# Block 2's inverse: norms earlier on VectorE, column steps on GpSimd

## The chip, the cores and the metric

The kernel runs on one core of a Trainium2 chip. The metric is device microseconds of one launch. TensorE (PE in the profile, PEld for its weight loads), VectorE (DVE), ScalarE (ACT), GpSimd (POOL) and SyncE (SP) each work through a queue of their own in order, and wait for each other by semaphores.

## The reference

Two stages follow each other: a delta-rule attention over 768 time steps for 32 (batch, head) pairs, and a mixture of experts that sends each token to one of 8 experts.

```python
k_n = k / (np.linalg.norm(k, axis=-1, keepdims=True) + 1e-06)
for t in range(S):                                   # S = 768, state is [4, 8, 48, 48]
    y[:, :, t] = np.einsum('bhd,bhde->bhe', q[:, :, t], state)
    v_old = np.einsum('bhde,bhd->bhe', state, kt)
    state = state + bt[:, :, :, None] * np.einsum('bhd,bhe->bhde', kt, vt - v_old)
# x = y as 3072 rows of 384
expert_idx = np.argmax(x @ w_gate, axis=1)
h = np.maximum(xe @ w1[e], 0.0)                      # for the rows xe of expert e
out[mask] = gate_w[mask, None] * (h @ w2[e])
```

## The kernel before

**Blocks and ticks.** The 768 steps are cut into 6 blocks of 128 (`NT`), tb = 0 to 5, and each block into four sub-blocks of 32. Inside a sub-block the recurrence becomes a triangular system, whose 32 x 32 inverse is needed for every pair and sub-block: 4 x 32 = 128 inverses in a block, one in each partition. The main loop runs over 27 ticks t (24 units of one batch of one block, and three to drain). In a tick four units are in flight, each at another of its four sub-blocks. A block's inverse must stand in the tile `wt` when its first unit enters, at tick 4 tb.

**A tick.** `residual(t)` multiplies keys with the state and with the rows just made (TensorE, L434 and L446, into `ks`); VectorE subtracts the result from `v_all` (L453); `apply(t)` multiplies by the inverses `wt` (TensorE, L461); ScalarE copies the result to `u` (L465); the next residual reads `u`. Around this chain stand the Gram matrices of later units (`kpart`, L271, `gg`), the queries' products (`qpart`: L281 on ScalarE, a mask L282 on GpSimd), outputs and states (`finish`), the gate's logits (`emit_x`, L528 to L530), the rows' scaling `scale_v` (L417 on VectorE) and the tokens' places (`pool_slots`, small GpSimd instructions, from the fifth tick on).

**The inverse of a block.** The diagonal 32 x 32 pieces of the Gram matrices go through DRAM (`gd`, L259, L263) into the tile `lg`. Then, on VectorE but for the square root:
- `squares` (L295) and `root` (L299, ScalarE): the keys' squared norms and their square roots;
- `prepare` (L317 to L341): nine short instructions, one on another, that make the norms and scale `lg`, with a copy of the norms by GpSimd (L346);
- 15 column steps (L369 for the first, then 14 pairs of L374, a product into `tmp`, and L377, its addition to `lw`) for the two 16 x 16 triangles on the diagonal;
- the corner: a copy (L382), six large products (L393, 784 to 1024 elements in each partition) and six sums (L399), which join the triangles, and the transpose into `wt` (L404).

**What sets the order.** All instructions are recorded by one Python program, and every engine runs its share in that order. A tick has seven places, and `beside(t, i)` runs at each (place number 7t + i). It records `squares` and `root` at the places that the first two numbers of `ROOT[tb]` name, and then inverse steps worth `SPEND` (0.86 to 0.92 us a place, by the program's own weights). Block tb's `prepare` may begin at the third number of `ROOT[tb]`. Where two blocks are under way the steps alternate between them, until the older one has its corner. What a block still lacks at tick 4 tb is recorded there, ahead of `residual`.

Of the kernel before, what the change touches and what calls it, by code (L numbers as in the profile page):

```python
# [13 lines left out]
ALU = mybir.AluOpType  # L14
# [27 lines left out]
def deltanet_moe(ctx, tc, kt_d, qt_d, kn_d, v_d, beta_d, w_gate, w1, w2, out):  # L42
    nc = tc.nc
# [76 lines left out]

    ROOT = {1: (-1, -1, -1), 2: (17, 20, 22), 3: (38, 41, 43), 4: (66, 69, 71), 5: (94, 97, 99)}
    INIT = (0, 1, 2, 3, 'l', 0)
# [233 lines left out]

    def lanes(tb):

# [3 lines left out]
        G, W = both_halves(lg), both_halves(lw)  # L362
        V = nc.vector
        tmp = fp.tile([128, 128], F32, name=f"tmp{tb}", tag=f"tmp{tb % 2}")
        for c in range(15):
            m, w = 15 - c, c + 1
            if c == 0:
                for g in (0, 16):
# [4 lines left out]
            x = tmp[:, 0:2 * m * w].rearrange("p (g a b) -> p g a b", g=2, a=m)  # L373
            V.tensor_tensor(out=x, in0=G(w, c, m, 1).broadcast_to([128, 2, m, w]),  # L374
                            in1=W(c, 0, 1, w).broadcast_to([128, 2, m, w]), op=ALU.mult)
            yield 0.2 + m * w / 480
            V.tensor_tensor(out=W(w, 0, m, w), in0=W(w, 0, m, w), in1=x, op=ALU.add)  # L377
            yield 0.2 + m * w / 480
        big = [fp.tile([128, 1024], F32, name=f"big{i}_{tb}", tag=f"big{i}") for i in range(2)]

# [24 lines left out]
        if tb + 2 < NT:  # L405
            clear_w(tb + 2)
        yield 2.0

    def scale_v(t, act=False):
# [524 lines left out]
    class Inverse:  # L934
# [6 lines left out]
        def steps(self):  # L941
            for _ in prepare(self.tb):
                yield 0.2
            yield 1.2
            self.at = 0
            yield from lanes(self.tb)

        def ready(self, t):
            if self.at == -12:
                return place[0] >= ROOT[self.tb][2]  # L950
            return not ("cols" in tiles[self.tb] and t < B * self.tb - 1)

        def step(self):
# [5 lines left out]
            return us  # L959

    line = [Inverse(tb) for tb in range(1, NT)]
    turn, owed, place = [None], [0.0], [-1]
# [6 lines left out]
    W = None  # L969

    def inverse_step(t):
# [7 lines left out]
        pair = ready and b is not None and "cols" not in tiles[a.tb]  # L979
        x = (b if turn[0] is a else a) if pair else a if ready else b  # L980
        turn[0] = x
# [18 lines left out]
    def beside(t, i):  # L1000

        place[0] = 7 * t + i
        for tb in ROOT:
            if place[0] == ROOT[tb][0]:
                squares(tb)
            if place[0] == ROOT[tb][1]:
                root(tb)
        inverses((SPEND0 if t < B else SPEND if t < 3 * B else SPEND2)[i], t)
        for _ in range(STEPS[i] if t < NN - B else 4):
            if fine and not run(fine[0]):  # L1010
                fine.pop(0)
# [343 lines left out]
```

## Time and profile before

| | us |
|---|---|
| median of 3 runs (lowest, highest) | 497.71 (496.09, 498.83) |
| profiled execution | 496.72 |
| its span in the trace | 495.0 |
| ticks 0 to 3 (40.59 to 70.12) | 29.53 |
| ticks 4 to 7 (70.12 to 105.64) | 35.52 |
| all ticks until the last subtraction (40.59 to 257.70) | 217.11 |
| the experts behind them (257.70 to 495.00) | 237.30 |
| busy over the span: PE, DVE, ACT, POOL | 453.5, 323.8, 262.1, 166.1 |

A tick is counted here from one L453 to the next, since each tick has one such instruction (some of the first and last have a narrower form). Busy PE time is modelled from pipelined matmuls; its idle time, with the engine that ended it in square brackets behind a row, is the surer number. An instruction that is held up by another engine's use of the memory shows as a longer instruction, not as idle time.

### The profile page before, as it was taken

The page shows a single profiled execution, that of the slowest core. Times are in us where ns is not written, and L with a number is a line of the kernel's source. Part 1 is how long each engine was busy: PE and PEld are TensorE (multiplying, and loading weights), DVE is VectorE, ACT ScalarE, POOL GpSimd, SP SyncE. Part 2 cuts the span into 40 slices and gives each one's busy share as a digit, 9 for nine tenths or more (in the row PEclk, how much of TensorE's full clock was granted, in tenths as well). Part 3 has the DMA queues.
Part 4 walks back from the last instruction along what each step waited for, and adds up shares of the span by engine and source line. Part 5 has one row for each costly group of instructions (what it writes and reads, how often), then busy time and mean ns, then how long its engine had stood idle before and what let it go on. Part 6 is the DMA issues. An engine that isn't in the chain of part 4 may idle for free. (4 is left out here: it accounts for less than half of the span.)

```text
span 495.0 us, 17216 instructions
## 1 busy us (share of the span) xinstructions
PE 453.5 (92%) x7212; PEld 417.3 (84%) x7212; DVE 323.8 (65%) x726; ACT 262.1 (53%) x566; POOL 166.1 (34%) x338
## 2 busy tenths in 40 slices
PE   6866799999999899978899999999999999999995
PEld 4755678887888687866798999999999999999995
DVE  3899998899889989446544767373463647255330
ACT  3464767675756466766433455463553545364230
POOL 7013123768888878730311210201102020201111
PEclk9998889999999999999999899999999999999999
DMA  5999478575384243734302548474545547353101
GB/s 164 246 291 252 126 156 254 169 162 168 88 206 106 86 131 89 234 121 128 101 35 66 168 139 248 140 223 132 177 124 171 175 150 199 138 170 106 36 3 46
DMA packets 57147, 73.33 MB, mean 148 GB/s; under 512 B 25929, under 2 KB 44831, under 8 KB 57056
## 3 DMA queue, kind: packets, MB, share of 16 engines
q1 hardware_dynamic: 53600, 62.44, 44.4%
q0 software_dynamic: 3456, 9.57, 5.3%
q8 instruction: 71, 1.16, 1.0%
q14 instruction: 20, 0.16, 0.1%
HBM read 54.15 MB, written 18.62 MB: 147 GB/s over the span
## 5 line engine op out<-in xcount | busy, mean ns | idle before, releaser
L801 POOL DMA_INDIRECT out_dram<-yo,idx x32 | 30.7, 959 | 198.7 <-ACT yo L1134 100.8
L798 PE MATMUL y<-w2h,hx 128*128 128x384 f32 x352 | 93.5, 340 | 0.1
L721 DVE TENSOR_TENSOR w2l<-w2r,w2h 128x768 fp32r<-128x768 f32 x32 | 31.2, 979 | 73.3 <-ACT w2h L720 73.2
L798 PEld LDWEIGHTS y<-w2h,hx 128*128 128x128 f32 x352 | 64.1, 188 | 0.4 <-issue 0.4
L798 PE MATMUL y<-w2l,hx 128*128 128x384 f32 x176 | 59.3, 337 | 0.0
L787 PE MATMUL h<-xl,w1h 128*128 128x416 f32 (+2 forms) x168 | 57.2, 341 | 0.2 <-DVE xl L721 0.2
L787 PE MATMUL h<-xh,w1h 128*128 128x416 f32 (+2 forms) x168 | 57.3, 341 | 0.0
L787 PE MATMUL h<-xh,w1l 128*128 128x416 f32 (+2 forms) x168 | 57.2, 340 | 0.0
L465 ACT COPY u<-ks 32x384 f32<-32x384 f32 x96 | 45.1, 469 | 21.0 <-PE ks L461 18.4
L282 POOL TENSOR_SCALAR_AFFINE_SELECT pm<-pm 128x1024 f32<-128x1024 f32 x24 | 27.1, 1130 | 75.9 <-ACT pm L281 75.5
L790 ACT ACTIVATE hx<-h 128x448 fp32r<-128x448 f32 (+1 forms) x64 | 32.9, 517 | 32.8 <-PE h L787 32.0
L1134 ACT ACTIVATE yo<-y,gt 128x384 f32<-128x384 f32 x22 | 12.8, 581 | 69.1 <-PE y L798 57.9
L434 PE MATMUL ks<-st,kt 128*32 128x96 f32 x768 | 45.1, 253 | 2.5 <-ACT u L465 2.1
L791 DVE SCALAR_TENSOR_TENSOR hx<-h,hx 128x448 fp32r<-128x448 f32 (+1 forms) x64 | 36.8, 587 | 14.5 <-ACT hx L790 14.4
L271 PE MATMUL pg<-kt 64*128 64x128 f32 x384 | 34.0, 319 | 8.0 <-DMA kt<-in_kt_dram 4.3
L271 PEld LDWEIGHTS pg<-kt 64*128 64x128 f32 x384 | 28.8, 219 | 12.4 <-ACT gg L253 6.4
L434 PEld LDWEIGHTS ks<-st,kt 128*32 128x32 f32 x768 | 33.2, 111 | 6.1 <-ACT u L465 2.6
L253 ACT COPY gg<-pg 128x512 f32<-128x512 f32 x48 | 25.8, 589 | 23.8 <-PE pg L271 23.8
L536 POOL DMA_INDIRECT xg<-row,sli x24 | 29.2, 1216 | 25.7 <-ACT yt L508 8.0
L461 PE MATMUL ks<-v_all,wt 32*32 32x48 f32 x1536 | 25.9, 203 | 12.9 <-DVE v_all L453 10.7
L461 PEld LDWEIGHTS ks<-v_all,wt 32*32 32x32 f32 x1536 | 21.3, 105 | 17.8 <-DVE v_all L453 12.6
L721 DVE TENSOR_TENSOR w1l<-w1r,w1h 128x1024 fp32r<-128x1024 f32 x24 | 29.4, 1224 | 9.8 <-ACT w1h L720 6.6
(197 smaller groups left out, 1040.5 us busy)
## 6 DMA issues: line engine op xcount, KB each, us to landing
w1r<-in_w_dram SPq DMA_DIRECT2D x24, 512.0 KB
w2r<-in_w_dram SPq DMA_DIRECT2D x32, 384.0 KB
xg<-zrow SPq DMA_DIRECT2D x7, 788.0 KB
kt<-in_kt_dram SPq DMA_DIRECT2D x17, 256.0 KB
xr<-xg SPq DMA_DIRECT2D x7, 591.0 KB
ku<-in_kn_dram SPq DMA_DIRECT2D x20, 192.0 KB
qt<-in_qt_dram SPq DMA_DIRECT2D x36, 96.0 KB
v_all<-in_v_dram SPq DMA_DIRECT2D x15, 192.0 KB
```

Source lines behind the costliest of these rows:

```text
L271: nc.tensor.matmul(pg[a][:, p], lhsT=kt[r, p], rhs=xt[r, p], start=True, stop=True, tile_position=(64 * a, 0), skip_group_check=True)
L282: nc.gpsimd.affine_select(out=pm, in_=pm, compare_op=ALU.is_gt, fill=0.0, base=0, pattern=[[0, H], [1, C]], channel_multiplier=-1)
L434: nc.tensor.matmul(ks[32 * q:32 * q + 32, 2 * p:2 * p + 2, :], lhsT=kt_t[n % KTL][:, p, 32 * q:32 * q + 32], rhs=st_view(n % B, p), start= ...
L461: nc.tensor.matmul(ks[r, h, :], lhsT=tiles[n // B]["wt"][r, n % B * H + h, :], rhs=vn[r, h, :], start=True, stop=True, tile_position=(32 * ...
L465: nc.scalar.copy(out=uview(n)[r], in_=ks[r])
L536: put = nc.gpsimd.indirect_dma_start(out=xg, out_offset=bass.IndirectOffsetOnAxis(ap=at, axis=0), in_=x, in_offset=None, bounds_check=OFF ...
L721: nc.vector.tensor_tensor(out=lo, in0=src, in1=hi.bitcast(F32), op=ALU.subtract)
L787: nc.tensor.matmul(ps, lhsT=w[:, d, fs], rhs=x_[:, d], start=(n == 0), stop=(n == len(terms) - 1))
L790: nc.scalar.activation(out=hh, in_=ps, func=AF.Relu)
L791: nc.vector.scalar_tensor_tensor(out=hl, in0=ps, scalar=0.0, in1=hh.bitcast(F32), op0=ALU.max, op1=ALU.subtract)
L798: nc.tensor.matmul(ps, lhsT=h(f)[h_], rhs=w2[w][:, f, :], start=(n == 0), stop=(n == len(terms) - 1))
L801: nc.gpsimd.indirect_dma_start(out=out, out_offset=bass.IndirectOffsetOnAxis(ap=idx, axis=0), in_=yo, in_offset=None, bounds_check=N - 1, ...
```

## The change

Block 2's `squares`, `root` and `prepare` come in tick 1, some ten places earlier than before, and while they last they are always taken ahead of the older block's steps. Its column steps 1 to 14 are recorded for GpSimd, two instructions at each place from place 13 (tick 1's last) on; its corner stays on VectorE and isn't recorded before place 29, tick 4's second. Blocks 3, 4 and 5 get their squares at places 30, 58 and 88 (38, 66 and 94 before). Nothing else is touched: TensorE, ScalarE and the DMA queues have the same instructions, ScalarE's root (L299) of blocks 2 to 5 stands earlier.

```diff
--- before.py
+++ after.py
@@ -118,7 +118,8 @@
     LAG = NB - 1
     FILL = 'k4 k5 k6 k7', 'k1 q0 k2 k3', 'k8 k9', 'k10 k11 q1'
 
-    ROOT = {1: (-1, -1, -1), 2: (17, 20, 22), 3: (38, 41, 43), 4: (66, 69, 71), 5: (94, 97, 99)}
+    ROOT = {1: (-1, -1, -1), 2: (7, 9, 11), 3: (30, 32, 34), 4: (58, 61, 63), 5: (88, 91, 93)}
+    COLS = {2: (13, 2, 1, 29)}
     INIT = (0, 1, 2, 3, 'l', 0)
 
     STEPS = (3, 3, 3, 2, 2, 2, 2)
@@ -354,13 +355,13 @@
             return bass.AP(tensor=t.tensor, offset=t.offset + 32 * r + c, ap=[list(t.ap[0]), [16 * 33, 2], [32, m], [1, w]])
         return view
 
-    def lanes(tb):
+    def columns(tb):
 
 
         T = tiles[tb]
         lg, lw = T["lg"], T["lw"]
         G, W = both_halves(lg), both_halves(lw)
-        V = nc.vector
+        V, P = nc.vector, nc.gpsimd if tb in COLS else nc.vector
         tmp = fp.tile([128, 128], F32, name=f"tmp{tb}", tag=f"tmp{tb % 2}")
         for c in range(15):
             m, w = 15 - c, c + 1
@@ -371,11 +372,17 @@
                 yield 0.4
                 continue
             x = tmp[:, 0:2 * m * w].rearrange("p (g a b) -> p g a b", g=2, a=m)
-            V.tensor_tensor(out=x, in0=G(w, c, m, 1).broadcast_to([128, 2, m, w]),
+            P.tensor_tensor(out=x, in0=G(w, c, m, 1).broadcast_to([128, 2, m, w]),
                             in1=W(c, 0, 1, w).broadcast_to([128, 2, m, w]), op=ALU.mult)
             yield 0.2 + m * w / 480
-            V.tensor_tensor(out=W(w, 0, m, w), in0=W(w, 0, m, w), in1=x, op=ALU.add)
+            P.tensor_tensor(out=W(w, 0, m, w), in0=W(w, 0, m, w), in1=x, op=ALU.add)
             yield 0.2 + m * w / 480
+
+    def corner(tb):
+
+        T = tiles[tb]
+        lg, lw = T["lg"], T["lw"]
+        V = nc.vector
         big = [fp.tile([128, 1024], F32, name=f"big{i}_{tb}", tag=f"big{i}") for i in range(2)]
 
         first_, prod = lg[:, 0:16, 0:16], lg[:, 0:16, 16:32]
@@ -405,6 +412,10 @@
         if tb + 2 < NT:
             clear_w(tb + 2)
         yield 2.0
+
+    def lanes(tb):
+        yield from columns(tb)
+        yield from corner(tb)
 
     def scale_v(t, act=False):
 
@@ -943,11 +954,18 @@
                 yield 0.2
             yield 1.2
             self.at = 0
-            yield from lanes(self.tb)
+            if self.tb in COLS:
+                held[self.tb] = columns(self.tb)
+                yield next(held[self.tb])
+                yield from corner(self.tb)
+            else:
+                yield from lanes(self.tb)
 
         def ready(self, t):
             if self.at == -12:
                 return place[0] >= ROOT[self.tb][2]
+            if self.tb in COLS and (self.tb in held or place[0] < COLS[self.tb][3]) and self.at == 1:
+                return False
             return not ("cols" in tiles[self.tb] and t < B * self.tb - 1)
 
         def step(self):
@@ -958,6 +976,15 @@
             self.at += 1
             return us
 
+    def columns_beside():
+
+        for tb in list(held):
+            n = ((place[0] - COLS[tb][0] + 1) * COLS[tb][1]) // COLS[tb][2] - ((place[0] - COLS[tb][0]) * COLS[tb][1]) // COLS[tb][2]
+            for _ in range(n if place[0] >= COLS[tb][0] else 0):
+                if tb in held and next(held[tb], None) is None:
+                    del held[tb]
+
+    held = {}
     line = [Inverse(tb) for tb in range(1, NT)]
     turn, owed, place = [None], [0.0], [-1]
 
@@ -977,7 +1004,7 @@
         if not ready and b is None:
             return None
         pair = ready and b is not None and "cols" not in tiles[a.tb]
-        x = (b if turn[0] is a else a) if pair else a if ready else b
+        x = (b if turn[0] is a or (b.tb in COLS and b.at < 0) else a) if pair else a if ready else b
         turn[0] = x
         return x.step()
 
@@ -1006,6 +1033,7 @@
             if place[0] == ROOT[tb][1]:
                 root(tb)
         inverses((SPEND0 if t < B else SPEND if t < 3 * B else SPEND2)[i], t)
+        columns_beside()
         for _ in range(STEPS[i] if t < NN - B else 4):
             if fine and not run(fine[0]):
                 fine.pop(0)
```

The line numbers of the changed kernel are 1 higher than before up to the column steps, 7 higher in the corner and 11 higher from `scale_v` on. In the rows below lg_443, lw_161 and big_1 are block 1's tiles, lg_604 and lw_633 block 2's; `x2` marks two instructions of one form.

VectorE from tick 1 (its subtraction reads ks_702) to tick 2 (ks_783 before, ks_793 after), before:

```order
L374 TENSOR_TENSOR tmp_678<-lg_443,lw_161 128x78
L377 TENSOR_TENSOR lw_161<-lw_161,tmp_678 128x2x3x13
L374 TENSOR_TENSOR tmp_678<-lg_443,lw_161 128x56
L377 TENSOR_TENSOR lw_161<-lw_161,tmp_678 128x2x2x14
L374 TENSOR_TENSOR tmp_678<-lg_443,lw_161 128x30
L377 TENSOR_TENSOR lw_161<-lw_161,tmp_678 128x2x15
L382 COPY lg_443<-lw_161 128x16x16
L393 TENSOR_TENSOR big_1_778<-lg_443 128x1024
L453 TENSOR_TENSOR v_all<-v_all,ks_783 96x384
```

After:

```order
L375 TENSOR_TENSOR tmp_678<-lg_443,lw_161 128x78
L378 TENSOR_TENSOR lw_161<-lw_161,tmp_678 128x2x3x13
L318 RECIPROCAL r_722<-s_721 128x32
L320 SCALAR_TENSOR_TENSOR r_722<-ss_720,r_722 128x32
L322 SCALAR_TENSOR_TENSOR s_721<-r_722,s_721 128x32
L324 RECIPROCAL r_722<-s_721 128x32
L326 TENSOR_TENSOR ss_720<-bl,r_722 128x32
L329 TENSOR_TENSOR lw_633<-ss_720,r_722 128x32
L333 SCALAR_TENSOR_TENSOR lg_604<-lg_604,lw_633 128x16x16 x2
L342 STREAM_TRANSPOSE r_722<-s_721 128x32
L464 TENSOR_TENSOR v_all<-v_all,ks_793 96x384
L370 TENSOR_SCALAR lw_633<-lg_604,lw_633 128x15 x2
```

The nine instructions of block 2's norms stand inside block 1's column steps and ahead of tick 2's subtraction, and the first column step of block 2 right behind it. Block 1's last two column steps, its copy and its first product come behind that subtraction. Block 2's squares (L296, not in the piece) stand right behind tick 1's subtraction.

VectorE from tick 3's subtraction to tick 4's, before:

```order
L393 TENSOR_TENSOR big_1_778<-lw_161,lg_443 128x960
L317 RECIPROCAL r_869<-s_868 128x32
L399 TENSOR_REDUCE lw_161<-big_1_779 128x4x16
L319 SCALAR_TENSOR_TENSOR r_869<-ss_867,r_869 128x32
L393 TENSOR_TENSOR big_1_779<-lw_161,lg_443 128x784
L321 SCALAR_TENSOR_TENSOR s_868<-r_869,s_868 128x32
L399 TENSOR_REDUCE lw_161<-big_1_778 128x5x16
L323 RECIPROCAL r_869<-s_868 128x32
L399 TENSOR_REDUCE lw_161<-big_1_779 128x7x16
L325 TENSOR_TENSOR ss_867<-bl,r_869 128x32
L404 STREAM_TRANSPOSE wt_1060<-lw_161 128x32x32
L453 TENSOR_TENSOR v_all<-v_all,ks_1064 128x384
```

After:

```order
L464 TENSOR_TENSOR v_all<-v_all,ks_917 128x384
L406 TENSOR_REDUCE lg_443<-big_1_847 128x5x16
L406 TENSOR_REDUCE lg_443<-big_1_846 128x7x16
L400 TENSOR_TENSOR big_1_847<-lw_161,lg_443 128x1024
L400 TENSOR_TENSOR big_1_846<-lw_161,lg_443 128x960
L406 TENSOR_REDUCE lw_161<-big_1_847 128x4x16
L400 TENSOR_TENSOR big_1_847<-lw_161,lg_443 128x784
L406 TENSOR_REDUCE lw_161<-big_1_846 128x5x16
L406 TENSOR_REDUCE lw_161<-big_1_847 128x7x16
L411 STREAM_TRANSPOSE wt_1099<-lw_161 128x32x32
L464 TENSOR_TENSOR v_all<-v_all,ks_1103 128x384
```

Between the two subtractions stand one product and two sums of block 1 more than before, and none of block 2's norms. The transpose into block 1's `wt` stays the last instruction ahead of tick 4's subtraction.

GpSimd from tick 1 on, before:

```order
L346 COPY nt_all<-r_628 32x32 x4
L423 MEMSET u_735 128x384
L423 MEMSET u_826 128x384
L282 AFFINE_SELECT pm_118<-pm_118 128x1024
L423 MEMSET u_951 128x384
L282 AFFINE_SELECT pm_119<-pm_119 128x1024
L288 MEMSET lw_1062 128x1024
L346 COPY nt_all<-r_869 32x32 x4
```

After:

```order
L434 MEMSET u_739 128x384
L347 COPY nt_all<-r_722 32x32 x4
L375 TENSOR_TENSOR tmp_823<-lg_604,lw_633 128x56
L378 TENSOR_TENSOR lw_633<-lw_633,tmp_823 128x2x14x2
L434 MEMSET u_842 128x384
L375 TENSOR_TENSOR tmp_823<-lg_604,lw_633 128x78
L378 TENSOR_TENSOR lw_633<-lw_633,tmp_823 128x2x13x3
L375 TENSOR_TENSOR tmp_823<-lg_604,lw_633 128x96
L378 TENSOR_TENSOR lw_633<-lw_633,tmp_823 128x2x12x4
L375 TENSOR_TENSOR tmp_823<-lg_604,lw_633 128x110
L378 TENSOR_TENSOR lw_633<-lw_633,tmp_823 128x2x11x5
L375 TENSOR_TENSOR tmp_823<-lg_604,lw_633 128x120
```

Block 2's 28 column instructions (L375 and L378) stand in this queue with two of the masks (L283) and two of the `u` memsets (L434) among them; before, only masks and memsets stood there until tick 4.

## Rows read from the trace of the kernel before

**Rows 1.** Busy time by stretch (start:end, length, then each engine's busy time, PEclk, DMA).
```profile
40.59:70.12 29.53, 23.25 (x539) 20.28 (x540) 28.19 (x64) 19.07 (x59) 4.79 (x11) 0.83 0.67 158
70.12:105.64 35.52, 33.89 (x960) 29.41 (x958) 30.49 (x76) 24.22 (x59) 20.57 (x49) 1.00 0.70 195
78.08:94.80 16.72, 16.20 (x469) 13.98 (x470) 14.21 (x34) 11.75 (x29) 10.06 (x26) 1.00 0.70 210
94.80:113.24 18.44, 16.61 (x472) 14.31 (x472) 17.09 (x40) 11.62 (x28) 13.06 (x32) 1.00 0.68 158
146.14:160.91 14.77, 13.91 (x438) 12.22 (x439) 14.33 (x31) 9.60 (x25) 11.89 (x24) 1.00 0.50 139
160.91:177.47 16.56, 14.21 (x437) 12.14 (x437) 14.83 (x38) 9.58 (x24) 13.29 (x33) 1.00 0.33 101
64.00:66.00 2.00, 2.00 (x31) 1.90 (x29) 2.00 (x5) 1.93 (x6) 0.00 (x0) 0.50 1.01 155
```

**Rows 2.** Timeline of PE: start, busy us, instruction [idle before it <- who ended that].
```profile
62.61 0.88 PE L461 MATMUL ks<-v_all,wt 32*32 32x48 f32 x64 [2.03 <-DVE v_all L453]
...
71.93 0.88 PE L461 MATMUL ks<-v_all,wt 32*32 32x48 f32 x64
...
106.23 0.88 PE L461 MATMUL ks<-v_all,wt 32*32 32x48 f32 x64 [1.00 <-DVE v_all L453]
...
171.61 0.88 PE L461 MATMUL ks<-v_all,wt 32*32 32x48 f32 x64 [1.45 <-DVE v_all L453]
```

**Rows 3.** Timeline of DVE, ticks 0 to 4.
```profile
41.04 0.32 DVE L317 RECIPROCAL r<-s 128x32 f32<-128x32 f32 x1
...
42.53 0.22 DVE L328 TENSOR_TENSOR lw<-ss,r 128x32 f32<-128x32 f32 x1
...
44.01 0.24 DVE L374 TENSOR_TENSOR tmp<-lg,lw 128x56 f32<-128x56 f32 x1
...
47.93 0.28 DVE L374 TENSOR_TENSOR tmp<-lg,lw 128x128 f32<-128x128 f32 x1
...
62.01 0.54 DVE L453 TENSOR_TENSOR v_all<-v_all,ks 128x384 f32<-128x384 f32 x1
...
68.26 2.04 DVE L404 STREAM_TRANSPOSE wt<-lw 128x1024 f32<-128x1024 f32 x1
70.12 0.56 DVE L453 TENSOR_TENSOR v_all<-v_all,ks 128x384 f32<-128x384 f32 x1
```

**Rows 4.** Timeline of SP's DMA issues, tick 1.
```profile
48.72 0.35 SPq L191 DMA_DIRECT2D kt<-in_kt_dram  x1
```

**Rows 5.** SP's waits from 36 to 52 us: in total, times, longest.
```profile
SPq L191 <- DMA lg<-gd: 1.2, 1, 1.2
```

**Rows 6.** Timeline of POOL and DVE where both read the memory.
```profile
59.92 1.09 POOL L282 TENSOR_SCALAR_AFFINE_SELECT pm<-pm 128x1024 f32<-128x1024 f32 x1 [14.41 <-ACT pm L281]
59.94 2.15 DVE L393 TENSOR_TENSOR big<-lw,lg 128x1024 f32<-128x1024 f32 x1
...
150.16 2.29 DVE L393 TENSOR_TENSOR big<-lg 128x1024 f32<-128x1024 f32 x2
150.28 1.16 POOL L640 TENSOR_TENSOR s<-oh 128x8 f32<-128x8 f32 x1
```

**Rows 7.** Timeline of POOL: small two-input instructions, and a memset.
```profile
108.07 0.22 POOL L679 TENSOR_TENSOR oh<-oh,beyond 128x16 f32<-128x16 f32 x1
108.38 0.22 POOL L681 TENSOR_TENSOR pos<-oh,pos 128x16 f32<-128x16 f32 x1
...
108.83 0.42 POOL L423 MEMSET u<- 128x384 f32 x1
```

**Rows 8.** Groups of instructions by line: busy us, mean ns of one | idle before.
```profile
L282 POOL TENSOR_SCALAR_AFFINE_SELECT pm<-pm 128x1024 f32<-128x1024 f32 x24 | 27.1, 1130 | 75.9 <-ACT pm L281 75.5
...
L374 DVE TENSOR_TENSOR tmp<-lg,lw 128x56 f32<-128x56 f32 (+3 forms) x84 | 24.6, 293 | 2.5
...
L377 DVE TENSOR_TENSOR lw<-lw,tmp 128x56 f32<-128x56 f32 (+3 forms) x84 | 21.7, 258 | 2.5
...
L85 POOL CAST ltri<-cmask 128x128 bf16<-128x128 f32 x1 | 0.3, 289 | 0.1
```

## The prediction, made before the changed kernel ran

> **What bounds the kernel now.** I read the busy time by stretch first, then the idle gaps of TensorE in the timeline, then VectorE's timeline ahead of each gap, and last the places where VectorE and GpSimd work at once.
>
> The stretches [rows 1] show two regimes. In ticks 0 to 3 VectorE is busy 28.19 of 29.53 us and TensorE only 23.25; GpSimd does 4.79. VectorE is still finishing block 1's inverse, which tick 4 needs. From tick 4 on TensorE is busy 33.89 of 35.52 us, so that only its idle time can be won. The idle that VectorE causes is in front of `apply` [rows 2]: 2.03 us at tick 3, none at tick 4, 1.00 at tick 8 and 1.45 at tick 16. Ticks 8 and 16 are where blocks 2 and 4 enter, and their transposes come late. At tick 4 there is a hidden margin: VectorE's subtraction starts at 70.12 and takes 0.56 [rows 3], but `apply` starts only at 71.93 [rows 2], since other matmuls stand ahead of it. So VectorE may be 71.93 - 70.68 = 1.25 us later at tick 4 at no cost, and after that TensorE pays in full.
>
> **The change part by part.**
>
> *Removed from VectorE.* 28 column instructions of block 2, 14 x (0.293 + 0.258) = 7.7 us [rows 8]. All of them stood in ticks 4 to 7, where VectorE is the engine that is waited for only at the end. With 7.7 us less there, and the norms of blocks 3 to 5 eight, eight and six places earlier, the transposes of blocks 2 and 4 are ready in time. What this gives back is TensorE's idle time at ticks 8 and 16, 1.00 + 1.45 = 2.45 us, by the gaps. By lengths it is more: ticks 7 and 8 together take 18.44 us against 16.72 for ticks 5 and 6 (1.72), and ticks 15 and 16 take 16.56 against 14.77 for 13 and 14 (1.79) [rows 1], 3.5 in all. I take the middle, -3.0.
>
> *Added ahead of block 1's transpose.* That chain on VectorE is nearly gapless until 70.12, so what is put into it moves tick 4.
> - (a) The end of block 2's norms and its first column step now come before it: in block 1 the same instructions took from 42.53 to 44.01 [rows 3], +1.5.
> - (b) The first five instructions of the norms were there already, but between large instructions; now they stand behind each other, each on the one before, as in block 1, where they took 42.53 - 41.04 = 1.49. If they were free before this adds 1.5, if equally dear 0. I take +0.5.
> - (c) The squares now stand right behind tick 1's subtraction, at 47.93 [rows 3]. They read `lg`, which comes by a DMA that SP waits for until 48.72 [rows 4, 5]. That is up to 0.8 of stall on VectorE. With the squares' own time I take +0.9.
> - (d) GpSimd's 28 instructions run while VectorE does block 1's last two column steps and six products, ten instructions with two inputs. The trace shows what happens when both read [rows 6]: the mask on GpSimd runs from 59.92 to 61.01, and the product that VectorE starts at 59.94 takes 2.15 instead of about 1.15 (two products back to back took 2.29). The other way round, a small GpSimd instruction that takes about 0.22 [rows 7] takes 1.16 beside a product. So they exclude each other. A GpSimd instruction of the new kind isn't in the trace. Below it stands the 16-element one at 0.22, above it memsets of 384 elements at 0.42 [rows 7]; a one-input instruction of 128 elements takes 0.289 and of 1024 1.13 [rows 8], which is 0.94 ns an element. The new ones have 30 to 128 elements, 95 in the mean, so I estimate 0.26 to 0.35, of which 0.1 to 0.3 keep VectorE out. Ten meetings at 0.25 are +2.5 (0 to 3.5).
> - (e) The 1.0 us that the mask cost the product at 59.94 may recur or not, since the mask now comes at another moment: -0.5 (0 to -1.0).
>
> The Trainium skill (SBUF — State Buffer, section Who interferes with whom) says that a VectorE instruction with two SBUF inputs contends with a GpSimd instruction that reads SBUF, that the loser waits for the whole instruction, and that a tensor_reduce never contends. The trace agrees [rows 6]; by the rule the six sums are free for GpSimd and (d) holds at its estimate, without it (d) would be 0.
>
> Sum: 1.5 + 0.5 + 0.9 + 2.5 - 0.5 = +4.9 us on VectorE at tick 4. The subtraction starts near 75.0 instead of 70.12, and less the margin of 1.25 `apply` comes 3.7 us later. Tick 3 itself changes little: there VectorE is later by (a) to (c) and part of (d), and earlier by the two sums and the product that have moved behind it.
>
> *What TensorE's longer waits cost besides.* After the 2.03 us gap at tick 3 the granted clock is 0.50 from 64 to 66 us [rows 1], that is 1.2 GHz. A gap of 2 to 3 us before tick 4 can bring the same a tick later, where TensorE is the bound. Such a stretch costs 0 (hidden) to 1.6 us; I take +0.6.
>
> *GpSimd's own queue.* Its steps start once VectorE has done the first column step, near 56. 28 instructions at 0.26 to 0.35, and 0.08 between two (108.07 to 108.38 for 0.22 [rows 7]), are 9.5 to 12 us; two masks and two memsets among them 2 x 1.13 + 2 x 0.42 = 3.1; six products hold one step each by up to 1.0, 6 at most. They end between 69 and 77. Block 2's corner starts with a copy that waits for the last of them, about 1.1 us after tick 4's subtraction, at 76.1. So I cost this wait at nothing, and it is the thinnest cover in the sum. Queued behind that copy are five products and sums, and tick 5's subtraction. The `u` memsets have a tick in hand, the masks three.
>
> Added up: +3.7 + 0.6 - 3.0 = +1.3 us. The profiled execution of 496.72 (span 495.0) becomes 498.0. The runs' median lies 1.0 above it at 497.71, so I predict 499.0.
>
> **The rivals.**
> - *GpSimd slips in for nothing.* For it: the small instructions ran at 0.22 with VectorE's column steps beside them [rows 7]. Against it: they have 16 elements, and the mask of 1024 did block. Then (d) is 0, `apply` is late by 4.9 - 2.5 - 1.25 = 1.2, no new gap lowers the clock, and the sum is 1.2 - 3.0 = -1.8: 495.9. With a stall in (c) of nothing as well it reaches 495.
> - *GpSimd is the bound of tick 5.* If a two-input step with short rows takes 0.5 us, 28 x 0.58 + 3.1 + 6 = 25.3 us, the steps end at 81.3 and the copy waits 5.2 us; 1.2 of it is hidden as at tick 4. The sum is 1.3 + 4.0 = +5.3: 503.0. It decides from about 0.36 a step on. For it: the masks in the same queue and the products that hold it; against it: the 0.94 ns an element [rows 8].
>
> The Trainium skill (GPSIMD Engine Reference, section 3.1) gives 4497 ns for a two-input instruction of 2048 elements. Worked out from that page my estimate is 0.2 us for 95 elements beside the fixed part, some 0.4 in all, which would put the end of the steps at 78.5 and the sum at +2.5. No run here shows such an instruction.
> - *The gains are hidden anyway.* If what waits at ticks 8 and 16 is taken over by another wait (the masks that block VectorE, or GpSimd's small instructions for the tokens), the -3.0 shrinks to -0.5 and the sum is +3.8: 501.5. For it: ticks 15 and 16 also contain a mask's collision; against it: VectorE has 7.7 us less to do in ticks 4 to 7.
>
> **How the numbers follow.** Half a per cent, 2.5 us, is what a measurement of this kernel can tell from no change; so faster means under 495.2 and slower over 500.2. The forecast has 0.45, with a range of its own from 497 to 501; GpSimd for nothing 0.25, GpSimd as the bound 0.15, hidden gains 0.15. Faster: half of the second case and, by the spread of the runs, a little of the first, 0.16. Slower: most of the last two and a quarter of the first, 0.36. The same: 0.48. The range from 495 to 503.5 takes in the ends of (d), the second case and most of the others.
>
> **What would show it.** In the profile after: VectorE's products and column steps of block 1 in ticks 2 and 3 longer than 1.15 and 0.29 us where a GpSimd column step overlaps them; tick 4's subtraction near 75 instead of 70.1; a TensorE gap of 2 us or more before `apply` at tick 4, and none at ticks 8 and 16; the copy L389 of block 2 with little idle time before it. I am wrong if the subtraction of tick 4 starts before 73, if the copy waits more than 1.5 us for GpSimd, or if gaps at ticks 8 or 16 stay.

## The result, and the profile after

The changed kernel took 505.76 us (median of 6 runs, 502.54 to 509.72) beside 498.27 for the kernel before: ratio 1.0141, 95% interval 1.0099 to 1.0184. Timed again on another occasion (12 runs) it was 1.0072 (1.0031 to 1.0113). So it is slower, by about 1% or 5 us; predicted were 499.0 us, +0.3%, and 505.76 lies outside the range of 495 to 503.5. The profiled execution after took 502.54 (span 500.8) against 496.72 (495.0); it is the fastest of the six runs, so the trace shows less than the median's loss.

The stretches that answer to [rows 1], in the same columns (length, then PE, PEld, DVE, ACT, POOL busy, PEclk), the last one for TensorE's clock behind tick 4:

```profile
40.74:75.17 34.43, 25.76 (x576) 22.68 (x576) 30.40 (x71) 21.12 (x62) 19.21 (x37) 0.83 0.60 148
75.17:110.66 35.49, 31.44 (x913) 27.32 (x913) 28.66 (x60) 21.75 (x53) 22.56 (x51) 0.95 0.67 181
85.94:102.47 16.53, 14.20 (x445) 12.26 (x446) 13.16 (x30) 10.36 (x26) 11.83 (x28) 1.00 0.48 150
102.47:120.32 17.85, 17.27 (x486) 15.21 (x488) 13.92 (x36) 12.12 (x30) 11.86 (x28) 1.00 0.69 167
153.17:167.41 14.24, 13.15 (x429) 11.21 (x430) 12.32 (x26) 8.90 (x22) 10.86 (x26) 1.00 0.44 130
167.41:183.70 16.29, 14.89 (x444) 13.02 (x444) 13.80 (x34) 9.47 (x24) 12.07 (x31) 1.00 0.35 113
76.00:80.00 4.00, 4.00 (x108) 3.52 (x96) 2.21 (x3) 2.50 (x6) 3.23 (x6) 0.57 1.06 288
```

Ticks 0 to 3 take 34.43 us on VectorE instead of 29.53, and VectorE is idle for 4.0 of them (1.3 before). Ticks 4 to 7 are as long as before, 35.49 to 35.52, although VectorE has 1.8 us less to do there: the time saved on VectorE turned into idle time. (It is 1.8 and not the 7.7 of block 2's column steps, mostly since 18 column instructions of block 3, with its earlier norms, now stand in these ticks.) Ticks 7 and 8 are 0.6 us shorter, 15 and 16 0.3.

TensorE's timeline at `apply` (ticks 2, 3, 4, 5, 8, 13 and 16), against [rows 2]:

```profile
57.33 0.88 PE L472 MATMUL ks<-v_all,wt 32*32 32x48 f32 x48 [2.74 <-DVE v_all L464]
63.95 0.88 PE L472 MATMUL ks<-v_all,wt 32*32 32x48 f32 x64
...
75.75 1.22 PE L472 MATMUL ks<-v_all,wt 32*32 32x48 f32 x64 [3.63 <-DVE v_all L464]
86.53 0.88 PE L472 MATMUL ks<-v_all,wt 32*32 32x48 f32 x64 [1.40 <-DVE v_all L464]
...
112.76 0.88 PE L472 MATMUL ks<-v_all,wt 32*32 32x48 f32 x64
...
153.77 0.88 PE L472 MATMUL ks<-v_all,wt 32*32 32x48 f32 x64 [1.23 <-DVE v_all L464]
...
176.64 0.88 PE L472 MATMUL ks<-v_all,wt 32*32 32x48 f32 x64
```

The gaps of ticks 8 and 16 are gone, as predicted, and the one of tick 3 has moved. In their place stand 2.74 at tick 2, 3.63 at tick 4, 1.40 at tick 5 and 1.23 at tick 13.

VectorE's timeline, against [rows 3]; what stands in brackets is its own idle time and who ended it:

```profile
48.38 0.55 DVE L464 TENSOR_TENSOR v_all<-v_all,ks 64x384 f32<-64x384 f32 x1 [0.78 <-PE ks L457]
50.60 0.19 DVE L296 TENSOR_SCALAR ss<-lg 128x32 f32<-128x32 f32 x1 [1.67 <-DMA lg<-gd]
...
65.87 3.38 DVE L400 TENSOR_TENSOR big<-lw,lg 128x1024 f32<-128x1024 f32 x2
...
75.17 0.53 DVE L464 TENSOR_TENSOR v_all<-v_all,ks 128x384 f32<-128x384 f32 x1
...
78.12 1.36 DVE L389 COPY lg<-lw 128x256 f32<-128x256 f32 x1 [1.76 <-POOL lw L378]
...
115.51 0.19 DVE L296 TENSOR_SCALAR ss<-lg 128x32 f32<-128x32 f32 x1 [1.77 <-DMA lg<-gd]
...
149.50 0.19 DVE L296 TENSOR_SCALAR ss<-lg 128x32 f32<-128x32 f32 x1 [0.83 <-DMA lg<-gd]
```

Four waits are new. Three are squares that wait for their `lg`, of blocks 2, 4 and 5; the fourth is the copy that waits for GpSimd's last column step. GpSimd's timeline, against [rows 6, 7]:

```profile
66.17 2.08 POOL L283 TENSOR_SCALAR_AFFINE_SELECT pm<-pm 128x1024 f32<-128x1024 f32 x1
68.22 1.33 POOL L375 TENSOR_TENSOR tmp<-lg,lw 128x128 f32<-128x128 f32 x1
...
72.02 0.40 POOL L375 TENSOR_TENSOR tmp<-lg,lw 128x120 f32<-128x120 f32 x1
...
77.84 0.25 POOL L378 TENSOR_TENSOR lw<-lw,tmp 128x30 f32<-128x30 f32 x1
```

A column step alone takes 0.25 to 0.45 us, beside a product about 1 us more, and the last ends at 78.1. The mask that collided at 59.94 before now collides at 66.17: the two products at 65.87 take 3.38 where two took 2.29 [rows 6].

To see where the loss arises I use TensorE's `apply` starts. This table gives, for one profiled execution of each kernel of the next section, the time in us between them:

| kernel | ticks 0 to 4 | 4 to 6 | 6 to 16 | 16 to 22 | ratio of the runs (95%) |
|---|---|---|---|---|---|
| before | 30.77 | 16.56 | 83.12 | 46.93 | 1 |
| change, first profile | 32.66 | 19.37 | 81.52 | 47.75 | 1.0141 (1.0099 to 1.0184) |
| change again | 31.95 | 20.48 | 82.41 | 47.56 | 1.0072 (1.0031 to 1.0113) |
| late roots | 34.21 | 19.24 | 82.05 | 48.19 | 1.0039 (1.0012 to 1.0067) |
| late corner | 33.16 | 18.47 | 83.50 | 48.08 | 1.0088 (1.0044 to 1.0132) |
| squares alone | 28.97 | 19.90 | 91.87 | 48.11 | 1.0176 (1.0118 to 1.0234) |
| columns late | 31.11 | 20.06 | 86.92 | 48.62 | 1.0129 (1.0088 to 1.0170) |
| scratch on GpSimd | 29.21 | 16.58 | 83.36 | 48.13 | 0.9961 (0.9931 to 0.9991) |
| late tick 4 | 34.51 | 17.66 | 83.17 | 49.94 | 1.0110 (1.0070 to 1.0150) |
| mended | 30.43 | 18.62 | 81.81 | 46.77 | 1.0017 (0.9981 to 1.0053) |
| masks behind | 28.96 | 21.21 | 83.08 | 46.79 | 1.0013 (0.9974 to 1.0052) |
| masks again | 28.46 | 17.77 | 83.66 | 48.75 | 0.9979 (0.9949 to 1.0009) |
| late norms | 28.11 | 18.21 | 85.85 | 47.51 | 1.0034 (0.9994 to 1.0074) |
| masks and budget | 28.47 | 17.88 | 81.58 | 48.87 | 0.9970 (0.9940 to 1.0001) |

The last stretch differs by up to 3 us among kernels that change nothing in it, so single profiles differ from each other by that much, and only the ratios decide between kernels. In both profiles of the change the loss is made up to tick 6 (4.7 and 5.1 us), and ticks 6 to 16 give 1.6 and 0.7 back.

### The profile page after: what moved, and what is told of

It is laid out like the page before. It is cut to its first block, busy times and chain, and to the rows that moved or that the text cites. A ratio compares the mean times of both kernels' runs of the same rounds, so it can differ in the third digit from the quotient of the medians.

```text
span 500.8 us, 17218 instructions
## 1 busy us (share of the span) xinstructions
PE 455.8 (91%) x7212; PEld 419.7 (84%) x7212; DVE 319.5 (64%) x698; ACT 262.1 (52%) x566; POOL 175.9 (35%) x366
## 3 DMA queue, kind: packets, MB, share of 16 engines
q8 instruction: 71, 1.16, 1.0%
HBM read 54.15 MB, written 18.62 MB: 145 GB/s over the span
## 5 line engine op out<-in xcount | busy, mean ns | idle before, releaser
L283 POOL TENSOR_SCALAR_AFFINE_SELECT pm<-pm 128x1024 f32<-128x1024 f32 x24 | 29.4, 1224 | 55.9 <-ACT pm L282 55.8
L445 PEld LDWEIGHTS ks<-st,kt 128*32 128x32 f32 x768 | 34.4, 114 | 6.0 <-ACT u L476 2.9
L547 POOL DMA_INDIRECT xg<-row,sli x24 | 27.9, 1162 | 25.6 <-ACT yt L519 8.1
```

Of the source, the lines that this page charges most:

```text
L283: nc.gpsimd.affine_select(out=pm, in_=pm, compare_op=ALU.is_gt, fill=0.0, base=0, pattern=[[0, H], [1, C]], channel_multiplier=-1)
L445: nc.tensor.matmul(ks[32 * q:32 * q + 32, 2 * p:2 * p + 2, :], lhsT=kt_t[n % KTL][:, p, 32 * q:32 * q + 32], rhs=st_view(n % B, p), start= ...
L547: put = nc.gpsimd.indirect_dma_start(out=xg, out_offset=bass.IndirectOffsetOnAxis(ap=at, axis=0), in_=x, in_offset=None, bounds_check=OFF ...
```

## The experiments

**Change again.** The changed kernel, unaltered.

> The changed kernel once more, unaltered, beside the kernel before and the other kernels of this stage. Theory: its loss does not hang on the chip it was first timed on; 1.009 to 1.018 of the kernel before, 4.5 to 9 us slower. Rival: a good part of that loss was that chip's; then 1.001 to 1.006, close to the change with the old places of blocks 3 to 5 (1.0039). In its trace the first waits of TensorE should again stand at ticks 2, 4 and 5 (about 2.7, 3.6 and 1.4 us), and VectorE should wait again for lg's transfer ahead of block 2's squares.

1.0072: slower again, between the two expectations. TensorE waits 3.70 us at tick 4 as in the first profile. The stall for `lg` stands at another place, with TensorE's wait behind it, and in tick 5's `apply` TensorE stands still for 2.00 us with no releaser in the trace ("issue"). TensorE, then VectorE:

```profile
73.19 1.50 PE L472 MATMUL ks<-v_all,wt 32*32 32x48 f32 x64 [3.70 <-DVE v_all L464]
...
86.41 0.23 PE L472 MATMUL ks<-v_all,wt 32*32 32x48 f32 x1 [2.00 <-issue]
...
120.67 0.88 PE L472 MATMUL ks<-v_all,wt 32*32 32x48 f32 x64 [2.45 <-DVE v_all L464]
```

```profile
114.35 0.19 DVE L296 TENSOR_SCALAR ss<-lg 128x32 f32<-128x32 f32 x1 [3.31 <-DMA lg<-gd]
...
120.08 0.54 DVE L464 TENSOR_TENSOR v_all<-v_all,ks 128x384 f32<-128x384 f32 x1
```

There is no wait for VectorE at tick 5, although the copy waited 2.13 us for GpSimd. Block 2's squares waited only 0.17 here, block 4's 3.31, and tick 9 is 2.45 late by it: how much each square waits varies from run to run.

**Late roots.** The change with the old places of blocks 3 to 5:

```
-    ROOT = {..., 3: (30, 32, 34), 4: (58, 61, 63), 5: (88, 91, 93)}
+    ROOT = {..., 3: (38, 41, 43), 4: (66, 69, 71), 5: (94, 97, 99)}
```

> The change, with the squares and norms of blocks 3, 4 and 5 at their old places. Theory A (three separate losses: VectorE's chain before tick 4, the copy's wait for GpSimd before tick 5, squares that wait for their DMA at ticks 8 and 12): VectorE's waits of 1.8 and 0.8 us for the DMA of blocks 4 and 5 go, the gaps before apply at ticks 13 and 17 shrink, the time falls by 1 to 2 us against the change's 505.8, a ratio to the kernel before of about 1.011. Theory B (the loss is TensorE's lower clock and the early ticks alone, what happens after tick 5 is hidden): no difference, ratio 1.014.

1.0039, below both expectations, against 1.0141 and 1.0072 with the new places. The interval lies apart from that of the first timing and overlaps that of the second, so it is likely, but not shown, that these places cost something of their own (0.3 to 1.0% by the ratios). Ticks 6 to 16 take 82.05 us, hardly other than in the change (81.52 and 82.41), although none of these three blocks' squares waits for its `lg` here. What stays up to tick 6 is not theirs.

**Late corner.** The change with block 2's corner held back to tick 5:

```
-    COLS = {2: (13, 2, 1, 29)}
+    COLS = {2: (13, 2, 1, 36)}
```

> The change, with block 2's corner not ahead of tick 5's second place, behind tick 5's subtraction. Theory A: VectorE's copy no longer waits 1.8 us for GpSimd ahead of that subtraction; the gap of 1.4 us before apply at tick 5 goes, the shift of apply against the kernel before stays near +3.8 at tick 5 instead of 6.4; the time falls by 2 to 3 us, a ratio of about 1.009. Theory B (tick 5 is late since TensorE runs at the lower clock after tick 4's gap): tick 5 stays late by 6, ratio 1.014.

1.0088, the ratio that theory A named, but not told apart from the change. The copy no longer stands ahead of tick 5's subtraction and TensorE has no gap there, yet tick 4 to tick 5 takes 10.19 us against 8.15. The stretch:

```profile
74.34:84.53 10.19, 10.19 (x233) 8.89 (x233) 3.95 (x15) 5.03 (x12) 5.13 (x9) 0.74 0.98 278
```

TensorE is busy without a break, at a mean granted clock of 0.74, while VectorE has 3.95 us of work: behind tick 4 it is the clock, not VectorE or GpSimd, that costs 2 us here.

**Squares alone.** The kernel before with the change's earlier places for blocks 3 to 5 and nothing else.

> The kernel before, with only the squares and roots of blocks 3, 4 and 5 at the change's earlier places (block 2 as before, no column step on GpSimd). Theory: these places cost by themselves about what taking them back gave, 1.006 to 1.010 of the kernel before (3 to 5 us), since the squares of blocks 4 and 5 wait on VectorE for lg's transfer (about 1 us each). Rival: they cost nothing of their own and bring what the prediction counted for them: the waits of 1.0 and 1.45 us ahead of ticks 8 and 16 go, 0.994 to 0.998 (1 to 3 us faster); the waits for lg then stand in the trace without a wait of TensorE behind them.

1.0176, worse than either expectation and than the whole change. The squares wait little (1.0 us in two). Most of the loss is at tick 8 (3.3 us more fall to ticks 4 to 6, with an issue gap of 1.72 in tick 5's `apply`). TensorE's and VectorE's timelines:

```profile
114.89 1.50 PE L461 MATMUL ks<-v_all,wt 32*32 32x48 f32 x64 [7.08 <-DVE v_all L453]
```

```profile
107.71 0.27 DVE L377 TENSOR_TENSOR lw<-lw,tmp 128x120 f32<-128x120 f32 x1
107.90 1.20 DVE L399 TENSOR_REDUCE lw<-big 128x64 f32<-128x1024 f32 x1
109.03 0.26 DVE L374 TENSOR_TENSOR tmp<-lg,lw 128x110 f32<-128x110 f32 x1
...
112.55 1.89 DVE L404 STREAM_TRANSPOSE wt<-lw 128x1024 f32<-128x1024 f32 x1
```

As soon as a block has its norms the scheduler alternates it with the one before. Block 3's column steps (L374, L377) now stand between block 2's products and sums, and block 2's transpose, due at tick 8, comes at 112.55 instead of 103.85. In the change this doesn't happen, since block 2's columns are out of VectorE's way. So the two parts of the change are tied: under this scheduler the early places need block 2's columns out of VectorE's way.

**Columns late.** All old places, the column steps on GpSimd in ticks 4 to 6 only:

```
-    COLS = {2: (13, 2, 1, 29)}
+    COLS = {2: (30, 2, 1, 45)}
```

> Norms of all blocks at their old places, block 2's column steps on GpSimd from tick 4 on, its corner not ahead of tick 6's fourth place. Theory A: ticks 0 to 4 are as before, nothing is added ahead of block 1's transpose; VectorE has little to do in ticks 4 and 5, block 2's transpose is ready in tick 7, so the gap of 1.0 us at tick 8 goes; 1 to 2 us faster than before, a ratio of 0.996 to 0.998. Rival (the exclusion follows the steps wherever they go): subtractions of ticks 4 to 7 late, gaps before apply there, ratio over 1.003.

1.0129: a miss. Ticks 4 to 6 lose 3.5 us (a wait of 2.57 at tick 4, then a granted clock of 0.71 to tick 5, and an issue gap of 1.36), ticks 6 to 16 another 3.8. In the latter GpSimd has its token work, and the small instructions of both stand in one queue beside products. TensorE ahead of tick 8, and two token instructions of GpSimd, which take about 0.2 us alone [rows 7]:

```profile
111.44 0.17 PE L677 MATMUL pp<-oh_all,ltri 128*128 128x16 bf16 x1 [5.27 <-POOL oh_all L673]
```

```profile
96.76 2.52 POOL L651 TENSOR_TENSOR sl_all<-s 128x2 f32<-128x2 f32 x1
...
105.26 2.43 POOL L658 TENSOR_TENSOR row<-rl,mx 128x16 f32<-128x16 f32 x1
```

**Scratch on GpSimd.** The kernel before, with 28 two-input instructions of 90 elements on scratch tiles in ticks 2 and 3 (and one of 16 elements ahead of them, which reads block 1's `lg`), so that only the sharing of the memory and the time in GpSimd's queue are added:

```
+            nc.gpsimd.tensor_tensor(out=scr, in0=esel[:, 0, 0:90], in1=esel[:, 1, 0:90], op=ALU.mult)
+            nc.gpsimd.tensor_tensor(out=scr, in0=esel[:, 2, 0:90], in1=scr, op=ALU.add)
```

> The kernel before, with 28 two-input instructions of 90 elements on GpSimd during ticks 2 and 3, on data that nobody needs; VectorE's work and order are those of before. Theory A (VectorE and GpSimd exclude each other when VectorE reads two inputs): the products of block 1 in ticks 2 and 3 take 0.2 to 0.4 us longer each, 1.5 to 2.5 in all, the subtraction of tick 4 comes that much later than 70.1, and the time is 0.5 to 1.5 us longer, since 1.25 of it is hidden; a ratio of 1.001 to 1.003. Rival (the small instructions slip between): products as before, tick 4 as before, ratio 1.000.

0.9961: not slower, even a little faster than before. VectorE and GpSimd side by side:

```profile
59.42 1.35 DVE L393 TENSOR_TENSOR big<-lw,lg 128x1024 f32<-128x1024 f32 x1
...
61.16 1.31 DVE L393 TENSOR_TENSOR big<-lw,lg 128x960 f32<-128x960 f32 x1
```

```profile
59.31 0.38 POOL L967 TENSOR_TENSOR scr<-esel 128x90 f32<-128x90 f32 x1
59.77 1.23 POOL L968 TENSOR_TENSOR scr<-esel,scr 128x90 f32<-128x90 f32 x1
...
62.66 1.09 POOL L282 TENSOR_SCALAR_AFFINE_SELECT pm<-pm 128x1024 f32<-128x1024 f32 x1
```

Whoever begins first holds the other: VectorE loses the 0.1 to 0.2 us that GpSimd's short instruction still has to run, GpSimd loses the rest of a product, 0.85 us. The gain has a likely source: the mask, pushed back to 62.66, now runs beside a sum, and the 1.0 us that it cost the product at 59.94 [rows 6] is saved.

**Late tick 4.** The kernel before, with VectorE kept busy for 5.20 us ahead of tick 4 (nine sums on scratch); nothing is moved, and GpSimd has no more to do.

```
+        for _ in range(9):
+            nc.vector.tensor_reduce(out=late, in_=esel[:, :, 0:96], axis=AX.X, op=ALU.add)
```

> The kernel before, with nine sums of 384 elements on a scratch tile put on VectorE ahead of the transpose of tick 4's inverse (some 4 us by the sums of its size in the trace), and nothing moved or put on GpSimd. Theory: what the change lost between ticks 4 and 6 (1.9 to 3.9 us beyond the 16.56 of before) follows from TensorE's long wait ahead of tick 4, not from GpSimd's queue or the copy that waits for it: here, too, TensorE waits 2 to 4 us, runs at a granted clock of 0.73 to 0.85 afterwards, and takes 10 us or so from tick 4 to tick 5 in place of 8.15; in all 1.006 to 1.012 of the kernel before. Rival: the loss behind tick 4 is the copy's wait and block 2's late corner, which this kernel does not have; then tick 4 to tick 6 stays within 0.5 us of 16.56 and the whole is 2 to 3 us slower or less (under 1.006).

1.0110, the size of the change's loss, with nothing moved to GpSimd. TensorE at tick 4, and the stretches behind it:

```profile
75.39 0.88 PE L461 MATMUL ks<-v_all,wt 32*32 32x48 f32 x64 [3.77 <-DVE v_all L453]
```

```profile
75.39:84.77 9.38, 9.38 (x233) 8.16 (x233) 7.37 (x28) 4.81 (x11) 3.59 (x8) 0.82 0.70 221
76.00:80.00 4.00, 4.00 (x77) 3.27 (x66) 3.66 (x16) 2.91 (x8) 1.57 (x5) 0.57 0.38 119
```

A wait of 3.77 us, then a clock of 0.57 from 76 to 80 us, exactly as in the change, and 1.2 us more from tick 4 to tick 5 than the 8.15 of before. So the low clock follows the long wait and needs nothing of GpSimd. The other profiles agree: the seven in which `apply` waits 2.57 to 3.77 us at tick 4 run to tick 5 at a granted clock of 0.71 to 0.84, the seven in which it waits 0.81 or less at 1.00. The loss is split otherwise than in the change, though: here 3.7 us are lost up to tick 4 and 1.1 in ticks 4 to 6, in the two profiles of the change 1.9 and 1.2 up to tick 4 and 2.8 and 3.9 behind it. So part of the theory's figure is missing. In the first profile the difference is the wait of 1.40 at tick 5; in the second, the issue gap of 2.00 and a low clock that cost 2.2 us instead of 1.2 behind a wait no longer than here; why it cost more isn't shown.

**Mended.** Old places for blocks 3 to 5, block 2's squares and columns three places later, its corner from place 36:

```
-    ROOT = {..., 2: (7, 9, 11), ...};    COLS = {2: (13, 2, 1, 29)}
+    ROOT = {..., 2: (10, 12, 14), ...};  COLS = {2: (16, 2, 1, 36)}
```

> The change with its squares and roots of blocks 3 to 5 at the old places, block 2's at 10, 12 and 14 of the list instead of 7, 9 and 11, the column steps on GpSimd from place 16 on and the corner from place 36 on. Theory: the stall of 1.67 us for lg in tick 1 and the earlier norms made tick 4 late, and both go: the stall is under 0.5 us, tick 4's application starts within 1.5 us of the kernel before, and the ratio is 0.998 to 1.003. Rival: GpSimd's steps, which then end some 2 us later still, hold up the copy and with it block 2's corner, so that tick 8 is late in place of tick 4: 1.004 to 1.010, with VectorE waiting over 2 us for lw ahead of the copy or TensorE over 1.5 us ahead of tick 8.

1.0017, no difference to be told from before: the loss of the change is gone, with GpSimd still doing all of block 2's columns. The squares at 50.23 have no wait at all. Subtraction to subtraction, ticks 0 to 4 take 31.13 us on VectorE (34.43 in the change, 29.53 before). Its work between ticks 4 and 5 fell to 1.52 us out of 9.30, and that still brings nothing. Not all of the loss behind tick 4 is gone: TensorE waits 3.10 us there, and ticks 4 to 6 take 2.1 us more than before; ticks 6 to 16 give 1.3 of it back.

**Masks behind.** The kernel before; two masks wait, by a 16-element instruction that reads a product, until block 0's second and block 1's fourth product are done.

```
+    HOLD = {0: (0, 1), 2: (1, 3)}
+            nc.gpsimd.tensor_tensor(out=dot, in0=t[:, 0:16], in1=t[:, 16:32], op=ALU.mult)
```

> The kernel before, with two of GpSimd's 1024-element masks (those of 25.33 and 59.92 us in the trace of before) held back by a 16-element instruction that reads the product they ran beside. Theory: a mask that begins first holds the product off for about 1 us, and both places lie on VectorE's path to tick 3: products of 1.15 us in place of 2.04 and 2.15, tick 3 about 1 us earlier, 0.9 to 2 us faster in all (0.996 to 0.998). Rival: the time is given back at tick 4, where TensorE and not VectorE came last (its margin there was 1.25 us), or the mask collides with the product behind: within 0.5 us (0.999 to 1.001).

1.0013, on the rival's side: the second mask moved onto the next product, and began 0.1 us before it. Even so ticks 0 to 4 take 1.8 us less than before; ticks 4 to 6 take 4.7 more, since TensorE stood still for 2.40 us in tick 5's `apply` and its mean granted clock from tick 5 to tick 6 was 0.74. VectorE, GpSimd and TensorE:

```profile
60.33 1.98 DVE L405 TENSOR_TENSOR big<-lw,lg 128x960 f32<-128x960 f32 x1
```

```profile
60.21 1.09 POOL L295 TENSOR_SCALAR_AFFINE_SELECT pm<-pm 128x1024 f32<-128x1024 f32 x1
```

```profile
80.56 0.28 PE L475 MATMUL ks<-v_all,wt 32*32 32x48 f32 x1 [2.40 <-issue]
```

**Masks again.** The same with `2: (1, 4)`, so that the mask falls beside sums.

> As the kernel with two masks held back, but the second mask waits for the product of 960 elements (the fifth of block 1) instead of the one of 1024, and so runs beside the sums behind it. Theory: no product of block 1 is then prolonged (1.15 us in place of 1.98 and 2.15), tick 4's subtraction comes 1.5 to 2 us earlier than before counted from tick 0's, TensorE's wait of 2.03 us ahead of tick 3 shrinks to about 1, and with it the low clock behind it; 0.994 to 0.998. Rival: what is saved ahead of tick 4 is lost again up to tick 9, where other waits come last: 0.998 to 1.002.

0.9979 (0.9949 to 1.0009), on the border of the two expectations. Ticks 0 to 4 take 2.3 us less than before; TensorE's wait at tick 3 falls from 2.03 to 1.10, and from tick 3 to tick 4 the clock is 1.00 instead of 0.82. The gain in the runs is smaller than that, and the interval still touches 1.

**Late norms.** Masks again, and block 2's norms behind tick 4, the other way round than the change: `2: (24, 26, 28)`.

> The kernel of the two held masks, and besides block 2's squares and roots at 24, 26 and 28 of the list (17, 20 and 22 before): the other way round than the change, with all of block 2's norms behind tick 4. Theory: work on VectorE ahead of tick 4 costs and work between ticks 4 and 6 is covered, so about 1.2 us less ahead of tick 4 makes it up to 1 us faster than the same kernel with the old places, and the later columns hide behind TensorE: 0.993 to 0.998 of the kernel before. Rival: block 2's corner comes late for tick 8, whose wait of 1.00 us grows by the delay of 2 to 3 us: 1.002 to 1.006.

1.0034 (0.9994 to 1.0074), the rival's side. Ticks 0 to 4 take least of all (28.11), but block 2's corner is late and tick 8 pays:

```profile
107.50 0.88 PE L475 MATMUL ks<-v_all,wt 32*32 32x48 f32 x64 [2.05 <-DVE v_all L467]
```

**Masks and budget.** Masks again, and the scheduler spends 1.0 instead of 0.9 us at each place of ticks 4 to 6, so that block 2's corner is drawn into VectorE's idle time there.

> The kernel of the two masks held back (the second behind the product of 960 elements), and besides the budget that the scheduler spends on inverses at each place of ticks 4 to 6 raised from 0.9 to 1.0 us; the kernel before in everything else. Theory: VectorE stood idle ahead of the subtractions of ticks 5 to 7 in before (1.21, 0.42 and 1.54 us) and was full ahead of tick 8 (9.43 of 9.43 us); with some 2 us of block 2's work drawn forward into that idle time, the wait of 1.00 us ahead of tick 8 goes, and nothing else moves: 0.5 to 1.5 us less than with the masks alone, 0.993 to 0.998 of the kernel before. Rival: the work drawn forward stands ahead of a subtraction that comes last, so that tick 5, 6 or 7 starts later by what tick 8 gains: 0.998 to 1.002.

0.9970 (0.9940 to 1.0001): the best of this series beside the scratch kernel, some 1.5 us, and not told apart from the masks alone. The step itself did what it should. TensorE at ticks 3 and 8, and the product and the mask:

```profile
61.04 0.88 PE L476 MATMUL ks<-v_all,wt 32*32 32x48 f32 x64 [1.10 <-DVE v_all L468]
...
103.96 0.88 PE L476 MATMUL ks<-v_all,wt 32*32 32x48 f32 x64
```

```profile
60.90 1.15 DVE L406 TENSOR_TENSOR big<-lw,lg 128x960 f32<-128x960 f32 x1
...
62.23 1.16 DVE L414 TENSOR_REDUCE lw<-big 128x64 f32<-128x1024 f32 x1
```

```profile
62.31 1.09 POOL L296 TENSOR_SCALAR_AFFINE_SELECT pm<-pm 128x1024 f32<-128x1024 f32 x1
```

The gap of tick 8 is gone, ticks 6 to 8 take 16.95 instead of 17.74 us, and a mask beside a sum prolongs neither.

## Why the prediction was wrong, point by point

Two steps failed most. For the stretch behind tick 4 the prediction had +0.6 us (the low clock) and nothing for GpSimd's wait; ticks 4 to 6 took 2.8 and 3.9 us more in the two profiles. The gains, put at -3.0, were 1.6 and 0.7. The delay ahead of tick 4 erred the other way: +3.7 forecast, 1.9 and 1.2 measured from `apply` to `apply`.

- **Where the work goes: right.** The prediction saw that ticks 0 to 3 are VectorE's and the later ones TensorE's, put +4.9 us on VectorE at tick 4 with the subtraction near 75.0, and it started at 75.17; `apply` was to come 3.7 us later and came 3.82 later. The gaps at ticks 8 and 16 went. Counted from tick 0, whose `apply` lay at 43.09 in that profile and at 41.16 before, the agreement is partly luck: over the four profiles of the change and its two close variants the subtraction is 2.6 to 4.9 us late, `apply` 1.2 to 3.4.
- **(c), the stall for `lg`: too small once.** 0.9 was taken; with the squares' own 0.19 the first profile has 1.86 (1.67 of wait), the second 0.36. The landing was read rightly from SP's wait [rows 4, 5], which ends with VectorE's in these profiles too; but it was taken from one profile, and it moves: 48.72 before, 50.60, 48.03, 49.34 and 49.18 in the change and its two close variants.
- **(d), the exclusion: too large, and the wrong side pays.** Ten meetings at 0.25 us were put on VectorE. The scratch kernel shows 0.1 to 0.2 a meeting on VectorE and about 0.85 on GpSimd, and in all no loss; in the change's first profile VectorE is busy 2.2 us longer in ticks 0 to 3, where (a), (b), (d) and (e) had added 4.0. (c) and (d) erred in opposite directions. What was (e), -0.5, didn't come: the mask met the products at 65.87 instead.
- **The low clock, +0.6: too small, and with the next point the largest miss.** From tick 4 to tick 5, with TensorE busy without a break, it cost 2.0 us in the late-corner kernel (10.19 for 8.15) and 1.2 in the late-tick kernel (9.38). The second profile of the change lost 2.2 (10.34). The prediction read the pattern in [rows 1] and then took less than half of its own upper price of 1.6; at tick 4 TensorE has no slack to hide it.
- **GpSimd's queue, "I cost this wait at nothing": failed.** The steps ended at 78.1, just outside the 69 to 77; the copy waited 1.76 us (2.13 in the second profile), over the 1.5 that the prediction had named as a sign of being wrong. TensorE waited 1.40 for it at tick 5 in the first profile, and not at all in the second or in the late corner, where the copy comes later. Single steps took 0.25 to 0.45 us, 0.38 in the mean where none was held up, so the rival's 0.36 was the truer mean. The Trainium skill (GPSIMD Engine Reference, section 3.1) had led to an estimate of some 0.4 us a step and an end at 78.5; the trace agrees with that, with 0.38 and 78.1.
- **The gains, -3.0: failed.** From tick 6 to tick 16 the two profiles gain 1.6 and 0.7 us. The two gaps went, but with the norms eight places earlier the prediction left out that the squares of blocks 4 and 5 read an `lg` that comes by the same kind of DMA as in (c). They now run ahead of its landing (waits of 1.77, 0.83 and 3.31 us), and ticks 9 or 13 wait in place of 8 and 16. That is the rival "gains are hidden anyway" with another wait in the role. It isn't the whole reason: in the late-roots kernel no square of blocks 3 to 5 waits and the gaps of ticks 8 and 16 are gone, and ticks 6 to 16 still gain only 1.1. No profile here gains more than 1.6 there, and what takes up the rest isn't shown: from tick 14 to tick 16, for one, the profile of before takes 16.67 us and the second of the change 16.71, with no gap ahead of tick 16. The argument that VectorE would have 7.7 us less to do in ticks 4 to 7 failed too: it had 1.8 less.

So with the measured sizes the sum is +1.9 up to tick 4, +2.8 from 4 to 6 and -1.6 from 6 to 16 for the first profile, +3.1 in all, and +1.2, +3.9 and -0.7 for the second: +4.4 instead of +1.3. The part between ticks 4 and 6 divides, by the idle time in the traces, into 1.4 of wait behind the copy and 1.2 of clock in the first profile, 2.2 of clock and 1.7 of issue gap in the second. Three things stay open: why the low clock costs 1.2 us in some profiles and 2.0 to 2.4 in others, where the median of the first timing lost 3 us more than its profiled run, and what the early places cost by themselves.

## What to carry to other kernels

Work taken off an engine is worth nothing where that engine is ahead, and work put ahead of a deadline costs more than what the waiting engine can't hide, if that engine comes back at a lower clock: 5.20 us of idle sums, of which 1.25 could be hidden, lost 3.7 us up to tick 4, 1.1 behind it, and as much as the change in all. Before moving an instruction earlier, look up when its input lands, for every block that moves and not only for the first. Where GpSimd shares the memory with VectorE, don't count meetings but ask which instruction begins first and how long it is: a 1024-element mask that begins just before a product is dear, short steps are nearly free for VectorE and dear for GpSimd's own queue.

## What the runs showed of the hardware that was not expected

- The exclusion has no favourite; in nearly all rows here the first comer wins: a mask of 1.09 us that began 0.02 to 0.12 us ahead of a product made it 1.98 to 2.15 us long, and a step that began after the product waited 0.8 to 1.0 us. In the columns-late kernel two instructions of 0.2 us waited 2.2 and 2.3, each over two products and a column step that followed each other, so the wait need not end with one product; and one of them had begun, by the trace, 0.05 us ahead of the product at 96.81, so starts as close as that don't settle who wins. Sums took no part: none of 1024 elements took over 1.22 us in any profile. The Trainium skill (SBUF — State Buffer, section Who interferes with whom) says of `tensor_reduce` that it doesn't contend; the sum of 1.16 us beside the mask of 1.09 agrees.
- In ten of the fourteen profiles TensorE stood still without a releaser in front of one and the same instruction, the last of the 64 matmuls of tick 5's `apply`: for 0.18 to 2.40 us. Two of them, of before and of masks again:

```profile
81.23 0.23 PE L461 MATMUL ks<-v_all,wt 32*32 32x48 f32 x1 [0.27 <-issue]
```

```profile
79.58 0.23 PE L475 MATMUL ks<-v_all,wt 32*32 32x48 f32 x1 [1.55 <-issue]
```

It took 1.3 of the 2.3 us that the masks had gained ahead of tick 4. Its cause was not tested.
